# A linear-attention and SwiGLU kernel: the attention's output projection of the last four token tiles as seven block products a pair

## The chip, the cores and the metric

The kernel runs on one core of one Trainium2 chip. The time is device microseconds from the start to the end of one execution; the median of three runs is quoted, with the lowest and the highest. Beside it one execution was recorded by the hardware profiler; its span runs from the first to the last instruction of the program and is a little shorter than the time of that execution. All starts below are microseconds from the start of that span.

Engine names: PE is the matrix engine (PEld its weight loads), DVE the vector engine, ACT the scalar engine, POOL is GpSimd, SP the engine that issues most of the DMAs. ACT issues some DMAs too; these stand in ACT's own stream of instructions, and an instruction that waits holds up all that stand behind it on the same engine.

## The reference

One block of 2048 tokens, width D = 1024, 32 heads of 32, and a feed-forward part with F = 3584:

```python
xn = _layernorm(x)
q, k, v = split(xn @ wqkv)                       # 32 heads of 32
phi = lambda t: where(t > 0, t + 1, exp(t)) + 1e-6
kv = einsum("bhsd,bhse->bhde", phi(k), v)
z  = einsum("bhsd->bhd", phi(k))
o  = einsum("bhqd,bhde->bhqe", phi(q), kv) / (einsum("bhqd,bhd->bhq", phi(q), z) + 1e-6)
s  = o.reshape(B, S, D) @ wo                     # the part that the change touches
g  = silu((silu(xn @ w_gate) * (xn @ w_up)) @ w_down)
return x + s * g
```

Inputs and the output are bfloat16.

## The kernel before

**Stages.** First the layer norm, k, v, q and the sums kv and z. Then a second stage, in the `with` block that opens the pools `wop`, `otp`, `work` and `small`, makes `o` and `s = o @ wo`. Then the feed-forward part (FFN), in which `Group` computes gate and up for 14 blocks of 256 columns, and a last stage that multiplies by `w_down` and writes the output.

**Block products.** Most large products are not done as eight block products of a 2x2 split but as seven (Strassen's scheme in Winograd's form): `part_a` does M3 into a PSUM tile X and M4 into Y, `part_b` does M1 into Z, M5 onto X and M2 onto Y, `part_c` does N7 onto X and N6 onto Y. Each block product is four matmuls of 128x512, all at line 131 (`products`). Between them ACT copies X out (`n` or `qu`), DVE adds Y and Z to it (`q`, `u`), ACT takes the finished off-diagonal blocks out of X and Y, and DVE subtracts N7's X and N6's Y from `u`. The operands are sums of blocks, made beforehand on DVE; for the FFN by `sum_w(m, gu)` (lines 152 to 155, four instructions for each of gate and up of column block m, into `ws_all[:, m % 2, gu]`). `sum_w` needs the raw weights, which `load_w(m)` fetches over SP's queue (lines 177 and 179, 512 KB each for `wg_sb` and `wu_sb`).

**The second stage.** There are 16 token tiles of 128, four to a block b. `emit_ND` computes `o` of one tile (eight small matmuls at line 790, the division on DVE at lines 794 to 800); `emit_OT` writes `o` to DRAM over ACT's queue (line 813) and reads it back transposed over SP's queue (line 814) into `oT_of(b)`: `oT_ab` for blocks 0 and 1, `oT_cd` for blocks 2 and 3, which lies in the storage of `wq_sb` and goes by that name in the trace. `emit_S(b, t, cc)` computes one half row tile of `s`: eight matmuls of 128x512 at line 827 into `s_ps`, an ACT copy to `s_sb` (line 831), and, after the second half, a store to `s_dram` over ACT's queue (line 834). `s_sb` has two buffers. There are 32 such units, u = 0 to 31; `units` and the sets `nd_at`, `row_at` and `q_at` say which other piece is emitted ahead of which unit. `row_at` places the last phi rows (lines 190 and 191, DVE) ahead of units 0 to 9. Ahead of unit 28 stand `sum_w(0, 0)` and `sum_w(0, 1)`, the operands of the first FFN groups. The order in this stage is the order of the code on PE, DVE, ACT, POOL and SP (`manual_schedule`); in the FFN only PE's and POOL's order is that of the code, and a scheduler places DVE's and ACT's instructions, so that instructions of the FFN can come to stand between the last ones of the second stage.

**Behind the last unit.** After the transpose of the last tile `emit_OT` issues the loads of column blocks 0, 1 and 2 of the FFN (`PREF = 3`), six transfers one behind the other on SP's queue. The FFN's first group takes its X, Y and Z from the PSUM space that the second stage leaves (`psF` after `psA` and `psB`; five `psB` tiles take turns). A DMA signals its end through one of eight DMA semaphores that SP's and ACT's transfers share in turn; a transfer that reuses a semaphore waits, on the engine that issues it, until the earlier transfer with that semaphore has landed.

Of the kernel before, what the change touches and what calls it, by code (L numbers as in the profile page):

```python
# [10 lines left out]
ALU = mybir.AluOpType  # L11
FP32 = mybir.dt.float32
# [9 lines left out]
def kernel(  # L22
# [11 lines left out]
    nc = tc.nc  # L34
# [45 lines left out]
    def gate(insts, after, sync=False):  # L80
        if after is None:
            return
        for d in insts:
            tc.add_manual_dep(d.ins, after.ins.name, SYNCD if sync else SCHED, reason="prefetch gate")
# [44 lines left out]
    def products(acc, lhs, rhs, n, first, c0=0, c1=CW):  # L129
        for k in range(n):  # L130
            marks["mm"] = nc.tensor.matmul(acc[:, 0:c1 - c0], lhsT=lhs(k), rhs=rhs(k)[:, c0:c1], start=(first and k == 0),  # L131
                                           stop=(k == n - 1), skip_group_check=True)
# [33 lines left out]
    def sum_w(m, gu):  # L166
        wsum[(m, gu)] = ws_all[:, m % 2, gu]
        for op in wsum_ops(wraw[(m, gu)], wsum[(m, gu)]):
            op()
# [18 lines left out]

    def emit_phi(dst, e):
        nc.vector.tensor_scalar(out=e, in0=e, scalar1=1.0, scalar2=EPS, op0=ALU.min, op1=ALU.add)  # L190
        nc.vector.tensor_tensor(out=dst, in0=e, in1=dst, op=ALU.add)

    p12 = ExitStack()
    wqp = p12.enter_context(tc.tile_pool(name="wqp", bufs=1))
# [16 lines left out]
    class QGroup:  # L211


        def __init__(self, p, m):
            w = wq_sb[:, :, m * FW:(m + 1) * FW]
            self.lhs, self.rhs = block_operands(w, ws_all[:, m // 2, m % 2]), x_operands(p)
            self.out = pqT_tiles[(p, m)]
            self.row = {}

        def mm(self, acc, which, first):  # L220
            products(acc, self.lhs[which], self.rhs[which], HD, first)
# [534 lines left out]
    with ExitStack() as p2:  # L756
        wop = p2.enter_context(tc.tile_pool(name="wop", bufs=1, reuse_waits="tile"))
        otp = p2.enter_context(tc.tile_pool(name="p2oT", bufs=1))
        work = p2.enter_context(tc.tile_pool(name="p2work", bufs=2))
        small = p2.enter_context(tc.tile_pool(name="p2small", bufs=2))  # L760
        oT_ab = otp.tile([P, 2, G, TB], BF16, name="oT")
        oT_cd = wq_sb[:].rearrange("p c n -> p (c n)").rearrange("p (b g t) -> p b g t", b=2, t=TB)
        s_tiles = {}
        wo_sb = wop.tile([P, G, D], BF16, name="wo_sb")

        def oT_of(b):
            return (oT_ab[:] if b < 2 else oT_cd)[:, b % 2]

        def emit_KVZ():
            for j in range(NJ):  # L770
                g0 = j * GPT
                ng = min(GPT, G - g0)
                nc.vector.tensor_tensor(out=KVZ[:, g0:g0 + ng, 0:P], in0=kvz_ps[j][:, 0:ng, 0:P],
                                        in1=mask[:, None, :].to_broadcast([P, ng, P]), op=ALU.mult)
                nc.vector.tensor_tensor(out=KVZ[:, g0:g0 + ng, P:P + HPG],
                                        in0=kvz_ps[j][:, 0:ng, P:P + 1].to_broadcast([P, ng, HPG]),
                                        in1=sel[:, None, :].to_broadcast([P, ng, HPG]), op=ALU.mult)

        def emit_ND(b, t):
            r0 = b * TB + t * P  # L780
            p, t0 = r0 // SP_TOK, r0 % SP_TOK
            nds = []
            rden = small.tile([P, G, HPG], FP32, name="rden", tag="rden")
            for j in range(NJ):
                g0 = j * GPT
                ng = min(GPT, G - g0)
                nd_ps = psA.tile([P, GPT, NDW], FP32, name="nd_ps", tag="A")
                for gi in range(ng):
                    g = g0 + gi
                    mm = nc.tensor.matmul(nd_ps[:, gi, :], lhsT=pqT_tiles[(p, g // 2)][:, g % 2, t0:t0 + P],  # L790
                                          rhs=KVZ[:, g, :], start=True, stop=True)
                    if j == 0 and gi == 0 and t == 0:
                        marks[("ND", b)] = mm
                nc.vector.tensor_scalar(out=rden[:, g0:g0 + ng, :], in0=nd_ps[:, 0:ng, P:P + HPG],
                                        scalar1=EPS, scalar2=None, op0=ALU.add)
                nds.append((g0, ng, nd_ps))
            nc.vector.reciprocal(out=rden[:], in_=rden[:])
            o_sb = work.tile([P, D], BF16, name="o_sb", tag="o_sb", bufs=4)
            for g0, ng, nd_ps in nds:
                nc.vector.tensor_tensor(  # L800
                    out=o_sb[:, g0 * P:(g0 + ng) * P].rearrange("p (g h e) -> p g h e", g=ng, h=HPG),
                    in0=nd_ps[:, 0:ng, 0:P].rearrange("p g (h e) -> p g h e", h=HPG),
                    in1=rden[:, g0:g0 + ng, :, None].to_broadcast([P, ng, HPG, DH]),
                    op=ALU.mult)
            o_ready.append((b, t, o_sb))

        o_ready = deque()

        def emit_OT():
            while o_ready:  # L810
                b, t, o_sb = o_ready.popleft()
                r0 = b * TB + t * P
                nc.scalar.dma_start(out=o_dram[r0:r0 + P, :], in_=o_sb[:])
                nc.sync.dma_start_transpose(out=oT_of(b)[:, :, t * P:(t + 1) * P], in_=o_dram[r0:r0 + P, :])
                if (b, t) == (NB - 1, TPB - 1):
                    for m in range(PREF):
                        load_w(m)

        def emit_S(b, t, cc):
            oT = oT_of(b)  # L820
            ttok = slice(t * P, (t + 1) * P)
            if (b, t) not in s_tiles:
                s_tiles[(b, t)] = work.tile([P, D], BF16, name="s_sb", tag="s_sb")
            s_sb = s_tiles[(b, t)]
            s_ps = psB.tile([P, CW], FP32, name="s_ps", tag="B")
            for c in range(G):
                mm = nc.tensor.matmul(s_ps[:], lhsT=oT[:, c, ttok], rhs=wo_sb[:, c, cc * CW:(cc + 1) * CW],  # L827
                                      start=(c == 0), stop=(c == G - 1))
                if c == 0:
                    marks[("S", b, t, cc)] = mm  # L830
            nc.scalar.copy(out=s_sb[:, cc * CW:(cc + 1) * CW], in_=s_ps[:])  # L831
            if cc == NCC - 1:
                r0 = b * TB + t * P
                nc.scalar.dma_start(out=s_dram[r0:r0 + P, :], in_=s_tiles.pop((b, t))[:])

        PREF = 3
        units = deque((b, t, cc) for b in range(NB) for t in range(TPB) for cc in range(NCC))
        nds = deque((b, t) for b in range(NB) for t in range(TPB))

        def s_unit():  # L840
            emit_S(*units.popleft())

        def nd_tile():
            if nds:
                emit_ND(*nds.popleft())

        with tc.manual_schedule(engines=FRONT_ORDER | {ET.SP}):

            qb, qc = QGroup(NPASS - 1, NM_Q - 2), QGroup(NPASS - 1, NM_Q - 1)
            for c in range(NCC):  # L850
                nc.sync.dma_start(out=wo_sb[:, :, c * CW:(c + 1) * CW], in_=wo_v[:, :, c * CW:(c + 1) * CW])
            emit_KVZ()
            qa.part_b()
            nd_tile()
            qb.part_a()
            emit_OT()
            qa.part_c()
            nd_tile()
            qb.part_b()
            emit_OT()  # L860
            nd_tile()
            qb.part_c()
            emit_OT()


            rows = deque((grp, i) for grp in (qa, qb, qc) for i in range(2))
            nd_at = {1, 2, 4, 6, 8, 10, 11, 13, 15, 16, 17, 19, 20}
            row_at = {0, 1, 3, 5, 7, 9}
            q_at = {0: qc.part_a, 2: qc.part_b, 3: qc.part_c}
            assert len(nd_at) == len(nds) and len(row_at) == len(rows)  # L870
            u = 0
            while units:
                if u in q_at:
                    q_at[u]()
                if u in nd_at:
                    nd_tile()
                if u in row_at:
                    grp, i = rows.popleft()
                    grp.part_d(i)
                if len(units) == 2 * NCC:  # L880
                    sum_w(0, 0)
                    sum_w(0, 1)
                s_unit()
                emit_OT()
                u += 1
    p12.close()
    ps12.close()

# [371 lines left out]
```

## Time and profile before

| | |
|---|---|
| time, median of 3 runs | 748.49 us (748.48 to 748.79) |
| the profiled execution: its time | 748.76 us |
| the profiled execution: its span | 747.0 us |
| granted PE clock | 0.999 of full speed |
| PE busy | 740.2 us, 3708 matmuls |
| DVE, ACT, POOL busy | 509.2, 273.4, 51.2 us |
| the four last token tiles' units, u = 24 to 31 | 219.69 to 233.5 us |
| HBM traffic over the span | 147 GB/s |

Busy times of engines overlap; the span is set by what PE does plus the stretches in which PE waits. A wait in brackets in the profile's lines, such as `[0.48 <-ACT s_sb L831]`, is idle time of that engine just before the instruction, and what ended it. An engine name with a q (SPq, ACTq) marks an instruction that issues a DMA; the time beside it is that of the issue, not of the transfer.

### The profile page before, as it was taken

Reading aid. Unit: us, or ns where it says so; the run is one execution under the profiler, and the core shown is the slowest. Engines: PE = TensorE matmul, PEld = TensorE weight load, DVE = VectorE, ACT = ScalarE, POOL = GpSimd, SP = SyncE. Lnnn points to the kernel's source line nnn. Section 1 sums busy time; section 2 is a strip of 40 time slices with the busy share of each in tenths; the row PEclk is TensorE's granted clock in tenths of the full one; section 3 lists DMA queues with packets and bytes.
Section 4 is the critical chain, followed back from the end, with each engine's and each line's share of the span. In section 5 each row is a group of like instructions: output and inputs, shape, how many; then the busy total and the mean of one; then the engine's idle time right before and its main releaser. Section 6 shows DMA issues by size and latency. Waiting matters only on the chain.

```text
span 747.0 us, 9899 instructions
## 1 busy us (share of the span) xinstructions
PE 740.2 (99%) x3708; PEld 347.8 (47%) x3708; DVE 509.2 (68%) x939; ACT 273.4 (37%) x478; POOL 51.2 (7%) x101
## 2 busy tenths in 40 slices
PE   9999999999999999999999999999999999999997
PEld 4544444455544444444444444444444444444454
DVE  6889896688735767886678867876655744445554
ACT  4444574755234334434343333434342111111111
POOL 3310000000000000000000000000000221121220
PEclk9999999999999999999999999999999999999999
DMA  9756000315799543655336643555879745554200
GB/s 318 253 163 168 1 0 1 113 44 160 195 230 276 148 140 104 185 178 161 103 102 198 190 123 106 152 157 161 260 247 349 291 169 183 183 183 183 85 29 29
DMA packets 132464, 118.09 MB, mean 158 GB/s; under 512 B 33728, under 2 KB 112704, under 8 KB 131136
## 3 DMA queue, kind: packets, MB, share of 16 engines
q1 hardware_dynamic: 127520, 108.68, 46.9%
q10 hardware_dynamic: 4896, 8.78, 3.5%
q8 instruction: 29, 0.48, 0.3%
q14 instruction: 19, 0.16, 0.1%
HBM read 70.52 MB, written 39.58 MB: 147 GB/s over the span
## 4 chain that ended last, share of the span: by engine, by line
PE 97%; DMA 1%; DVE 1%; ACT 0%; issue 0%; ACTq 0%; DVEq 0%
PE X L131 29%; PE Y L131 29%; PE Z L131 10%; PE kv_ps L455 9%; PE s_ps L827 6%; PE qY L131 3%; PE qX L131 3%; PE kY L131 2%; PE kX L131 2%; DMA wg_sb<-in_B_w_gate_dram 1%; PE nd_ps L790 1%; PE kvz L484 1%; PE qZ L131 1%; PE w_ps L493 1%; PE kZ L131 1%; PE tr_ps L411 0%
## 5 line engine op out<-in xcount | busy, mean ns | idle before, releaser
L131 PEld LDWEIGHTS <-ws_all 128*128 128x128 bf16 x1420 | 137.7, 98 | 162.3 <-issue 0.2
L923 DVE TENSOR_TENSOR q<-n,Y 128x512 f32<-128x512 f32 x63 | 43.3, 687 | 106.1 <-PE Y L131 106.1
L131 PEld LDWEIGHTS <-xs 128*128 128x128 bf16 (+1 forms) x736 | 69.6, 98 | 76.5
L1193 POOL TENSOR_TENSOR o_out<-y,xres 128x512 bf16<-128x512 f32 x29 | 35.2, 1213 | 663.3 <-DVE y L1192 663.3
L131 PE MATMUL Y<-xs,ws_all 128*128 128x512 f16 (+3 forms) x308 | 70.3, 360 | 0.0
L131 PE MATMUL X<-xnT,ws_all 128*128 128x512 f16 (+1 forms) x280 | 70.2, 379 | 0.0
L131 PE MATMUL X<-xs,ws_all 128*128 128x512 f16 x224 | 57.5, 379 | 0.0
L131 PE MATMUL Z<-xs,ws_all 128*128 128x512 f16 x224 | 57.5, 379 | 0.0
L131 PE MATMUL Y<-xnT,ws_all 128*128 128x512 f16 x224 | 57.5, 379 | 0.0
L1047 ACT ACTIVATE g<-cg 128x512 bf16<-128x512 f32 x56 | 35.3, 631 | 54.1 <-DVE cg L938 54.0
L929 DVE TENSOR_TENSOR u<-Z,q 128x512 f32<-128x512 f32 x63 | 43.1, 685 | 16.0 <-PE Z L131 15.9
L1047 ACT ACTIVATE g<-X 128x512 bf16<-128x512 f32 x28 | 16.7, 597 | 99.5 <-PE X L131 99.5
L455 PEld LDWEIGHTS <-xnT 128*128 128x128 f16 x320 | 30.7, 98 | 35.8 <-DVE xnT L427 0.5
L919 ACT COPY n<-X 128x512 f32<-128x512 f32 x63 | 36.9, 585 | 28.4 <-PE X L131 27.7
L1072 DVE TENSOR_TENSOR ho<-g,up 128x1024 bf16<-128x1024 bf16 x56 | 38.1, 684 | 0.5
L455 PE MATMUL kv_ps<-wk_sb,xnT 128*128 128x512 bf16 x160 | 37.3, 379 | 0.3 <-DVE xnT L427 0.3
L455 PE MATMUL kv_ps<-wv_sb,xnT 128*128 128x512 bf16 x160 | 36.5, 379 | 0.0
L1192 DVE TENSOR_TENSOR y<-y,s_in 128x512 f32<-128x512 f32 x31 | 22.2, 716 | 20.9 <-ACT y L1186 15.8
L131 PEld LDWEIGHTS <-wg_sb 128*128 128x128 bf16 x224 | 21.9, 98 | 27.1 <-issue 0.8
L131 PEld LDWEIGHTS <-wu_sb 128*128 128x128 bf16 x224 | 21.9, 98 | 26.4
L831 ACT CAST s_sb<-s_ps 128x512 bf16<-128x512 f32 x32 | 18.5, 585 | 40.0 <-PE s_ps L827 36.1
L1186 ACT ACTIVATE y<-X 128x512 f32<-128x512 f32 x8 | 4.8, 597 | 69.7 <-PE X L131 69.7
(179 smaller groups left out, 1132.6 us busy)
## 6 DMA issues: line engine op xcount, KB each, us to landing
h_dram<-ho SPq DMA_DIRECT2D x56, 256.0 KB, 2.6
wg_sb<-in_B_w_gate_dram SPq DMA_DIRECT2D x14, 512.0 KB, 4.1
wu_sb<-in_B_w_up_dram SPq DMA_DIRECT2D x14, 512.0 KB, 4.2
wdr<-in_B_w_down_dram SPq DMA_DIRECT2D x14, 512.0 KB, 4.1
ws_all<-h_dram SPq DMA_DIRECT2D x4, 1792.0 KB, 8.6
wds_dram<-wdsA SPq DMA_DIRECT2D x14, 384.0 KB, 2.7
hp_a<-h_dram SPq DMA_DIRECT2D x3, 1792.0 KB, 8.9
o_dram<-o_sb ACTq DMA_DIRECT2D x16, 256.0 KB, 3.1
```

The lines of the kernel that those rows point to most:

```text
L131: marks["mm"] = nc.tensor.matmul(acc[:, 0:c1 - c0], lhsT=lhs(k), rhs=rhs(k)[:, c0:c1], start=(first and k == 0), stop=(k == n - 1), skip_g ...
L455: mm = nc.tensor.matmul(kv_ps[:], lhsT=xn_tok_ap(i)[:, dc, :], rhs=wkv_ap(c)[:, dc, :], start=(dc == 0), stop=(dc == DC - 1))
L484: nc.tensor.matmul(kvz_ps[j][:, gi, 0:P + 1], lhsT=pk_sb[:, g * P:(g + 1) * P], rhs=v_sb[:, g, 0:P + 1], start=(i == 0 and gi == 0), stop= ...
L827: mm = nc.tensor.matmul(s_ps[:], lhsT=oT[:, c, ttok], rhs=wo_sb[:, c, cc * CW:(cc + 1) * CW], start=(c == 0), stop=(c == G - 1))
L831: nc.scalar.copy(out=s_sb[:, cc * CW:(cc + 1) * CW], in_=s_ps[:])
L919: nc.scalar.copy(out=n[:], in_=self.X[:])
L923: nc.vector.tensor_tensor(out=self.q[:], in0=n[:], in1=self.Y[:], op=ALU.add)
L929: nc.vector.tensor_tensor(out=self.u[:], in0=Z[:], in1=self.q[:], op=ALU.add)
L1047: nc.scalar.activation(out=self.g[:, i, j * TB:(j + 1) * TB], in_=src, func=ACT.Silu)
L1072: nc.vector.tensor_tensor(out=self.ho[:, i], in0=self.g[:, i], in1=self.up[:, i], op=ALU.mult)
L1192: nc.vector.tensor_tensor(out=t[:], in0=t[:], in1=self.s_in[:, i, cs], op=ALU.mult)
L1193: (nc.vector if last and (i, j) != (0, 0) else nc.gpsimd).tensor_tensor(out=self.o_out[:, i, cs], in0=t[:], in1=self.xres[:, i, cs], op=AL ...
```

## The change

The last four token tiles (block 3) are no longer done as eight units but as two pairs of tiles, each pair a 256-row product of seven block products (`SGroup`, with the same three parts as the other groups). A pair's left operands are sums of blocks of `oT`, made on DVE by `sums()` (four instructions a pair); the right operands are sums of blocks of `wo`, made once, on GpSimd, by five instructions of 128x2048, emitted ahead of units 10, 11, 12, 14 and 18 and made to wait for the last phi row (`marks["phi"]`). The sums lie in storage that is free by then: `oT_ab` of blocks 0 and 1, the second half of `ws_all`, and `oT_cd` of block 2. `s_sb` has four buffers in place of two. `sum_w(0, 0)` and `sum_w(0, 1)` move from ahead of unit 28 to behind `part_c` of the first pair and behind `part_c` of the second. `load_at` only renames the place of the loads.

```diff
     def emit_phi(dst, e):
...
-        nc.vector.tensor_tensor(out=dst, in0=e, in1=dst, op=ALU.add)
+        marks["phi"] = nc.vector.tensor_tensor(out=dst, in0=e, in1=dst, op=ALU.add)
...
-                s_tiles[(b, t)] = work.tile([P, D], BF16, name="s_sb", tag="s_sb")
+                s_tiles[(b, t)] = work.tile([P, D], BF16, name="s_sb", tag="s_sb", bufs=4)
...
+        wo_sums = deque((out, u, v, op) for out, (u, v, op) in zip(wos, (
+            (w12, w22, ALU.subtract), (w21, w11, ALU.subtract), (w11, w22, ALU.add), (w21, w22, ALU.add),
+            (w11, w12, ALU.add))))
+        s_rhs = {"M3": wos[0], "M4": wos[1], "M1": wos[2], "M5": w22, "M2": w11, "N7": wos[3], "N6": wos[4]}
...
+        class SGroup:
...
+            def sums(self):
+                o, sm, tt = self.o, self.sum, nc.vector.tensor_tensor
+                a, b = slice(0, P), slice(P, 2 * P)
+                tt(out=self.s1, in0=o[:, 0:HD, a], in1=o[:, HD:DC, b], op=ALU.add)
+                tt(out=sm[:, :, 0:2 * P], in0=o[:, 0:HD, :], in1=o[:, HD:DC, :], op=ALU.add)
+                tt(out=sm[:, :, 2 * P:3 * P], in0=o[:, HD:DC, b], in1=o[:, HD:DC, a], op=ALU.subtract)
+                tt(out=sm[:, :, 3 * P:4 * P], in0=o[:, 0:HD, a], in1=o[:, 0:HD, b], op=ALU.subtract)
...
+            def store(self, i):
+                r0 = ((NB - 1) * TPB + self.t + i) * P
+                nc.scalar.dma_start(out=s_dram[r0:r0 + P, :], in_=self.s[i][:])
+
+            def part_a(self):
+                self.s = [work.tile([P, D], BF16, name="s_sb", tag="s_sb", bufs=4) for _ in range(2)]
+                self.X = psB.tile([P, CW], FP32, name="sX", tag="B")
+                self.mm(self.X, "M3", True)
+                self.u = qtmp.tile([P, CW], FP32, name="qu", tag="qu")
+                nc.scalar.copy(out=self.u[:], in_=self.X[:])
+                self.Y = psB.tile([P, CW], FP32, name="sY", tag="B")
+                self.mm(self.Y, "M4", True)
+                nc.vector.tensor_tensor(out=self.u[:], in0=self.u[:], in1=self.Y[:], op=ALU.add)
+
+            def part_b(self):
+                Z = psB.tile([P, CW], FP32, name="sZ", tag="B")
+                self.mm(Z, "M1", True)
+                nc.vector.tensor_tensor(out=self.u[:], in0=self.u[:], in1=Z[:], op=ALU.add)
+                self.mm(self.X, "M5", False)
+                nc.scalar.copy(out=self.out(0, 1), in_=self.X[:])
+                self.mm(self.Y, "M2", False)
+                nc.scalar.copy(out=self.out(1, 0), in_=self.Y[:])
+
+            def part_c(self):
+                for acc, which, i in ((self.X, "N7", 0), (self.Y, "N6", 1)):
+                    self.mm(acc, which, False)
+                    nc.vector.tensor_tensor(out=self.out(i, i), in0=self.u[:], in1=acc[:], op=ALU.subtract)
+                    self.store(i)
...
+            wo_at = {10, 11, 12, 14, 18}
+            sum_at = {23: lambda: groups[0].sums()}
...
-            while units:
+            n7 = TPB * NCC
+            groups = [SGroup(t) for t in range(0, TPB, 2)]
+            for u in range(len(units) - n7):
...
-                if len(units) == 2 * NCC:
-                    sum_w(0, 0)
-                    sum_w(0, 1)
+                if u in wo_at:
+                    out, a, b, op = wo_sums.popleft()
+                    gate([nc.gpsimd.tensor_tensor(out=out, in0=a, in1=b, op=op)], marks["phi"], sync=True)
+                if u in sum_at:
+                    sum_at[u]()
                 s_unit()
                 emit_OT()
-                u += 1
+            sg, sh = groups
+            sg.part_a()
+            sh.sums()
+            sg.part_b()
+            sh.part_a()
+            sg.part_c()
+            sum_w(0, 0)
+            sh.part_b()
+            sh.part_c()
+            sum_w(0, 1)
```

## The prediction

> **What bounds the kernel now.** Read first were the page's busy times, its slices and its chain of waits.
>
> ```profile
> span 747.0 us, 9899 instructions
> PE 740.2 (99%) x3708; PEld 347.8 (47%) x3708; DVE 509.2 (68%) x939; ACT 273.4 (37%) x478; POOL 51.2 (7%) x101
> ...
> PE 97%; DMA 1%; DVE 1%; ACT 0%; issue 0%; ACTq 0%; DVEq 0%
> ```
>
> PE sets the time: 97% of the chain, at a granted clock of 0.999. So a matmul that goes is worth its place in PE's stream, and a wait of PE costs its length, if nothing later takes it back. Next came the timeline from 200 to 242 us, the end of the second stage and the start of the FFN (columns: start, duration, engine, line, operation, and in brackets the idle time before it and what ended it).
>
> ```profile
> 212.78 20.88 PE L827 MATMUL s_ps<-wo_sb,wq_sb 128*128 128x512 bf16 x96
> ...
> 221.73 0.63 SPq L179 DMA_DIRECT2D wu_sb<-in_B_w_up_dram  x1
> ...
> 223.95 0.33 ACTq L834 DMA_DIRECT2D s_dram<-s_sb  x1
> ...
> 227.32 0.42 DVE L152 TENSOR_TENSOR ws_all<-wg_sb 128x512 bf16<-128x512 bf16 x1 [12.40 <-DMA wg_sb<-in_B_w_gate_dram]
> ...
> 231.04 0.43 DVE L152 TENSOR_TENSOR ws_all<-wu_sb 128x512 bf16<-128x512 bf16 x1 [2.03 <-DMA wu_sb<-in_B_w_up_dram]
> ...
> 231.32 1.07 ACT L831 CAST s_sb<-s_ps 128x512 bf16<-128x512 f32 x2 [3.95 <-DMA s_dram<-s_sb]
> ...
> 233.34 0.43 DVE L152 TENSOR_TENSOR ws_all<-wg_sb 128x512 bf16<-128x512 bf16 x1 [0.60 <-DMA wg_sb<-in_B_w_gate_dram]
> ...
> 233.49 1.03 PE L131 MATMUL X<-xs,wg_sb 128*128 128x512 f16 x4
> ...
> 235.00 1.02 PE L131 MATMUL Y<-xs,wg_sb 128*128 128x512 f16 x4 [0.48 <-ACT s_sb L831]
> ...
> 235.24 0.43 DVE L152 TENSOR_TENSOR ws_all<-wu_sb 128x512 bf16<-128x512 bf16 x1 [0.20 <-DMA wu_sb<-in_B_w_up_dram]
> ...
> 236.86 0.68 DVE L923 TENSOR_TENSOR q<-n,Y 128x512 f32<-128x512 f32 x1
> ...
> 237.59 1.02 PE L131 MATMUL Y<-xnT,ws_all 128*128 128x512 f16 x4
> ```
>
> The reader is to see four things. PE runs through units 20 to 31 without a gap. The weights that the FFN needs arrive only just in time: the four DVE rows at line 152 give the landings of gate 0, up 0, gate 1 and up 1 as 227.3, 231.0, 233.3 and 235.2. ACT was stopped for 3.95 us by a store whose `s_sb` buffer it wanted, and through that PE lost time at the FFN's Y (Y starts 1.51 us after X, where four matmuls take 0.86: 0.65 lost). And the last row above, the FFN's first M2 at 237.59, stands right behind the end of `q` at 237.54, so both PE and DVE's chain from the landing of up 1 end there. I take that M2 as the marker: from there on PE has no gap in the old trace, so its shift is the shift of the span.
>
> **What is removed.** Twelve units take 20.88 us, 1.73 each (the last matmul's tail of 0.16 left off). Eight units are 13.8 us; two pairs are 2 x 7 block products of 0.863, 12.1 us. Gain 1.73. Four `s_sb` buffers take away the wait for the old store; with it the loss of 0.65 at Y goes. If nothing else waited, M2 would stand at 219.69 + 12.08 + 4 x 0.863 = 235.23, 2.36 us earlier.
>
> **What is added on POOL.** Five sums of 128x2048. The nearest row is line 1193, 128x512 in 1213 ns mean, so 4.9 us each; its slowest row took 2.81, so 11.2 as upper bound; below 4 x 1.15 nothing speaks for. I take 4.9. The last phi row ends at 191.06; four sums then end at 210.7, and the fifth, which must also wait for block 1's last unit (203.3), at 215.6. The first use is M3 at 219.69, the last N6 at 226.60. This is hidden, with 9 us and more to spare; where it is not, see below. Contention of POOL with DVE: in the last stage DVE's subtractions from PSUM (line 938) keep about 0.68 us beside POOL, and a sum of two SBUF operands (line 1159) rises from 1.08 to 1.66 in its longest. From 191 to 215 DVE has only the division of `o`, whose large operand is in PSUM; I take nothing.
>
> **What is added on DVE and on the transposes' times.** The sums of a pair are four instructions, by the rows of lines 152 to 155 in pitches of 0.34, 0.60, 0.34 and 0.34. A pair needs its second tile at once, so the transposes count: they landed at 219.63 for tile 1 (issued 214.18, 5.4 us) and 222.9 for tile 3 (issued 219.54, 3.4). Tile 1 is first used by M4 at 220.55, tile 3 at 224.87. Slack 0.9 and 2.0 us: no wait. DVE runs pair 1's sums to 221.3, pair 2's from 222.9 to 224.6, then u + Z, the next u + Y and pair 1's two subtractions, the last one done at 228.3. PE goes on to pair 2's M2 at 229.19 without a wait.
>
> **What is moved, and where the wait goes.** Two queues decide. The first is ACT's. In the built program the store of tile 0 reuses the DMA semaphore of gate 0's load, that of tile 1 up 0's, that of tile 2 gate 1's, that of tile 3 up 1's. Before, up 0's landing held no store. Now the store of tile 1, in ACT's stream ahead of pair 2's two copies out of X and Y, waits for it, and PE's N7 of pair 2 waits for the copy. The second is DVE's. In the built program its order at the border is:
>
> ```
> pair 1: u - X, u - Y
> sum_w gate 0: lines 152 153 154 155
> pair 2: u + Z
> sum_w gate 1: lines 152 153        <- waits for gate 1's load
> pair 2: u - X
> sum_w gate 1: line 154
> pair 2: u - Y
> sum_w up 0: lines 152 153 154 155
> sum_w gate 1: line 155 ; sum_w up 1: line 152
> FFN q (needed by the FFN's first M2)
> ```
>
> So everything down to `q` is queued behind the landing of gate 1; the FFN's Z also waits for u - Y of pair 2.
>
> When do these loads land? The store of tile 0, issued at 223.95 before, can't leave ahead of 227.5 now (it waits for N7's result and for gate 0). It landed after 7.3 us, in the middle of up 0 and gate 1. In 227.3 to 231.0 the DMAs moved 312 GB/s, so 256 KB (0.26 MB) are 0.84 us: up 0 lands at 230.2 and gate 1 at 232.5. If gate 1 follows up 0 as up 1 followed gate 1 (1.9 us), it lands at 232.1. I take 232.3. The ends are 231.6 (the stores of tiles 0 and 1 both out of the way, 233.3 less twice 0.84) and 233.3 (nothing gained).
>
> ACT: store 230.2 + 0.33, copy 0.58 and some 0.1 of hand-over: N7 starts at 231.2, 1.15 later than 230.05. The second stage ends at 232.9 in place of 231.8. DVE from gate 1's landing: 0.34 + 0.60 (lines 152, 153), 0.60 (u - X; pitch of line 938), 0.34, 0.60 (u - Y), 0.34 + 0.60 + 0.34 + 0.34 (up 0), 0.34, 0.34, then `q` 0.68 and 0.05 to PE: 5.5 us. M2 starts at 232.3 + 5.5 = 237.8, against 235.23 with no wait and 237.59 before. The FFN's Z isn't late: u - Y ends at about 234.9, PE is there at 234.7.
>
> **Sum.** +0.2 us on the span of 747.0: the 2.36 of gain are given back, 1.15 at pair 2's N7 and the rest at M2. The profiled execution took 748.76, 0.27 above the median of the runs; the same shift on the median 748.49 gives 748.7. With the two ends of the landing M2 lies at 237.1 and 238.8, that is -0.5 and +1.2: 748.0 to 749.7.
>
> One rule of the Trainium skill bears on the landing. The traced store needed 7.3 us for 256 KB, so it stood behind what SP had already queued. The skill's page "DMA: Bandwidth & Descriptors", section "Queues, rings and completion order", says that each DMA engine takes turns between the rings of SP and ACT, packet by packet; a store would then not stand behind the loads. The traced 7.3 us speak against it, though not strictly.
>
> **Rivals.**
>
> *The stores compete at once.* Mechanism in this kernel: tile 0's store, issued at 227.5, takes its 0.84 us from up 0 and gate 1 just as the old one did, so gate 1 lands at 233.3 as before. M2 at 238.8, +1.2 us: 749.7. For it: stores issued at 212.99 and 217.04 landed in 3.3 and 3.0 us beside other traffic. Against it: the two stores among the loads took 7.3 and 6.2. The Trainium skill's rule of turns, above, would give this one.
>
> *The gain arrives.* M2 near 235.2 to 236: 746.1 to 746.9. It needs gate 1 to land before 230.6 and up 0 before 229.5, each 1.5 us or more earlier than in the old trace, or another order on DVE than the built one. For it: PE's stream is otherwise free, and the loads lose a competitor. Against it: 1.57 MB ahead of that landing, of which only 0.26 to 0.5 MB can get out of the way.
>
> *Slower.* One mechanism: gate 1's load lands later than before, because both stores of pair 1 (0.5 MB, 1.7 us of DMA) now fall in the same 3 us as it, at 227.5 and 230.2, where before the first was spread over 7 us. From 233.6 on the kernel is slower by over 1.5 us, and each us later costs one us; at 234 to 235 M2 is at 239.5 to 240.5: +1.9 to +2.9, 750.4 to 751.4. For it: DVE has no way round that landing. Against it: SP issues the loads earlier than these stores.
>
> *POOL too slow.* At 11.2 us a sum the fourth ends at 235.9 and the fifth at 247.1, where N6 wants it at 226.6: 20 us, some 769. It decides from 8.7 us a sum (four sums between 191.06 and N7 at 225.73). Only the first POOL instruction of that kind in the last stage took so long.
>
> That the products aren't saved is no rival: the built program has eight matmuls less.
>
> **Chances.** Forecast 0.48, stores compete at once 0.13, gain arrives 0.19, slower 0.17, POOL 0.03. A change of 0.2%, 1.5 us, is about what a measurement of this kernel tells from none. The first two lie within it (0.61), faster has 0.19, slower 0.20. The likeliest's own range is 748.0 to 749.7; 8 in 10 needs most of the case that gains and the near half of the slower one: 746.3 to 750.7.
>
> **What would show it.** In the new trace: ACT idle until about 230.2 for a DMA of `wu_sb` and N7 of pair 2 late behind it; DVE idle ahead of line 152 on the second `wg_sb`, and M2 of the FFN at its landing plus 5.5. POOL's five sums done by 216. It would be wrong if PE waits for POOL, if M4 or pair 2's M3 wait for a transpose, or if DVE reaches `q` by 235.

## The result and the profile after

The changed kernel takes 747.89 us (median of 22 runs, 747.15 to 748.88) where the kernel before, run beside it, takes 748.92 (748.34 to 749.57). The ratio is 0.9986, with an interval of 0.998 to 0.9993: 0.14% faster, or 1.0 us. The forecast was +0.2 us, the range 746.3 to 750.7. So the time is inside the wide range, but just below the likeliest case's own (748.0 to 749.7). It is within 0.2% of no change, but the sign is the other one, and the interval lies wholly below 1. Of the 1.73 us that the products promised, and of the 2.36 with the waits, 1.0 came through.

First the page of the changed kernel: its span, the busy times and the shares of the chain of waits.

```profile
span 746.2 us, 9886 instructions
...
PE 736.9 (99%) x3661; PEld 347.0 (47%) x3700; DVE 517.4 (69%) x955; ACT 272.3 (36%) x476; POOL 69.9 (9%) x106
...
PE 96%; DMA 2%; DVE 1%; issue 0%; ACT 0%; DVEq 0%; ACTq 0%
```

PE still sets the time. Weight loads fell from 3708 to 3700, the eight matmuls saved (of the matmul records of this trace 39 are missing). POOL is busy for 19 us more.

Then the timeline of the changed kernel around the border of the two stages (start, duration, engine, line, operation; in brackets the idle time before it and what ended it).

```profile
219.91 1.03 PE L131 MATMUL sX<-oT,wq_sb 128*128 128x512 bf16 x4
...
227.78 1.83 ACTq L884 DMA_DIRECT2D s_dram<-s_sb  x2
227.88 0.69 DVE L908 TENSOR_TENSOR s_sb<-qu,sY 128x512 bf16<-128x512 f32 x1 [0.17 <-PE sX L131]
...
229.40 1.03 PE L131 MATMUL sY<-wo_sb,wq_sb 128*128 128x512 bf16 x4
...
229.71 0.58 ACT L901 CAST s_sb<-sX 128x512 bf16<-128x512 f32 x1 [3.83 <-PE sX L131]
...
230.34 1.02 PE L131 MATMUL sX<-ws_all,wq_sb 128*128 128x512 bf16 x4
...
231.30 0.42 DVE L152 TENSOR_TENSOR ws_all<-wg_sb 128x512 bf16<-128x512 bf16 x1 [0.53 <-DMA wg_sb<-in_B_w_gate_dram]
231.64 0.68 DVE L153 TENSOR_TENSOR ws_all<-wg_sb 128x1024 bf16<-128x1024 bf16 x1
...
232.07 1.03 PE L131 MATMUL X<-xs,wg_sb 128*128 128x512 f16 x4
232.24 0.68 DVE L908 TENSOR_TENSOR s_sb<-qu,sX 128x512 bf16<-128x512 f32 x1
...
232.93 1.03 PE L131 MATMUL Y<-xs,wg_sb 128*128 128x512 f16 x4
...
233.18 0.68 DVE L908 TENSOR_TENSOR s_sb<-qu,sY 128x512 bf16<-128x512 f32 x1
...
233.91 1.02 PE L131 MATMUL Z<-xs,ws_all 128*128 128x512 f16 x4
...
234.94 1.02 PE L131 MATMUL X<-xnT,ws_all 128*128 128x512 f16 x4
...
236.05 0.68 DVE L1011 TENSOR_TENSOR q<-n,Y 128x512 f32<-128x512 f32 x1
...
236.79 1.02 PE L131 MATMUL Y<-xnT,ws_all 128*128 128x512 f16 x4 [0.83 <-DVE q L1011]
```

Read it from the bottom. The FFN's first M2 is at 236.79, with PE idle for 0.83 us ahead of it, for `q` on DVE. Going up DVE's column, `q` ends a run without a gap that begins at 231.30 with the first sum of gate 1, and that one was released by the DMA of `wg_sb`. The busy time of each engine in that stretch says the same (window, length, then busy time and instructions of PE, PEld, DVE, ACT and POOL, TensorE's granted clock, DMA share, GB/s):

```profile
231.30:236.79 5.49, 4.66 (x22) 1.85 (x21) 5.49 (x13) 2.46 (x3) 0.00 (x0) 1.00 1.13 337
```

DVE is busy for 5.49 of 5.49 us, PE for 4.66. This is the chain that the prediction wrote down, at its length (5.5). What came out otherwise is the time at which it begins.

The whole change of the span can be read between two marks: the start of the last four tiles on PE and that M2. Before: 219.69 to 237.59, 17.90 us. After: 219.91 to 236.79, 16.88 us. The difference, 1.02 us, is close to that of the medians, 1.03, but the agreement is in part chance: two further profiles of the kernel before, below, have 17.57 and 17.27 between these marks, and a second one of the changed kernel 16.67, so a single pair of profiles gives anything from 0.4 to 1.2. The size of the gain is that of the medians; the marks show where it lies. The other 0.2 between the two profiled spans (747.0 and 746.2) lies ahead of the first mark, where executions of one kernel differ as well (219.7 to 220.1 in the three of the kernel before). From M2 to the end both take 509.4 us, so nothing is taken back later. PE without any wait would need 12.08 + 3.45 = 15.53 us between the marks. So the changed kernel loses 1.35 there: 0.08 at pair 2's N7 (230.34), 0.12 and 0.17 at the FFN's Z and the X behind it, 0.99 at M2 (each the distance of two starts less 0.863).

Last, the groups of POOL's instructions, in the view by lines of the changed kernel (busy us, mean ns, then the idle time before them):

```profile
L959 POOL TENSOR_TENSOR oT<-wo_sb 128x2048 bf16<-128x2048 bf16 x3 | 12.2, 4072 | 147.2 <-DVE pqT L191 147.2
L959 POOL TENSOR_TENSOR ws_all<-wo_sb 128x2048 bf16<-128x2048 bf16 x2 | 8.1, 4082 | 0.0
```

The five sums of `wo` take 4.07 us each and end at 211.5, over 8 us ahead of the last four tiles.

### The profile page after: what moved, and what is told of

Read it like the earlier page. It is cut to its first block, busy times and chain, and to the rows that moved or that the text cites. A ratio compares the mean times of both kernels' runs of the same rounds, so it can differ in the third digit from the quotient of the medians.

```text
span 746.2 us, 9886 instructions
## 1 busy us (share of the span) xinstructions
PE 736.9 (99%) x3661; PEld 347.0 (47%) x3700; DVE 517.4 (69%) x955; ACT 272.3 (36%) x476; POOL 69.9 (9%) x106
## 4 chain that ended last, share of the span: by engine, by line
PE 96%; DMA 2%; DVE 1%; issue 0%; ACT 0%; DVEq 0%; ACTq 0%
PE X L131 29%; PE Y L131 29%; PE Z L131 10%; PE kv_ps L455 9%; PE s_ps L829 5%; PE qX L131 3%; PE qY L131 3%; PE kY L131 2%; PE kX L131 2%; DMA wg_sb<-in_B_w_gate_dram 1%; PE nd_ps L790 1%; PE kvz L484 1%; PE qZ L131 1%; PE kZ L131 1%; DMA xp<-in_A_x_dram 0%
## 5 line engine op out<-in xcount | busy, mean ns | idle before, releaser
L829 PE MATMUL s_ps<-wo_sb,oT 128*128 128x512 bf16 x123 | 29.0, 379 | 0.2
```

## The experiments

The theory under test: the chain of DVE behind gate 1's landing is all that stands between the changed kernel and 15.53 us, and the landing itself varies between executions. Rivals: the stores of pair 1 among the loads set the landing; the four row tiles are the gain, or a part of it; POOL's sums take time from DVE or PE.

### The changed kernel again

Nothing is edited.

> The changed kernel once more, as the neighbour of the next three. Theory (the gain is cut by DVE's chain, which waits for the load of gate 1): the FFN's first M2 starts 5.5 us behind the landing of gate 1, wherever that falls; with a landing between 231 and 233 M2 is at 236.6 to 238.5 and the span 746.0 to 747.9. Rival (M2 is bound by PE's own stream or by the pairs' own work): M2 keeps its distance to the end of the second stage, 4.7 us behind the start of X, and does not follow the landing.

747.47 us (11 runs), ratio 0.9983, interval 0.9974 to 0.9992. In its profile gate 1 lands at 231.00 and M2 stands at 236.58, again 5.58 behind the landing, and 16.67 behind the first mark. So the sign is no accident of one job, and M2 follows the landing as expected.

### FFN's sums of gate 1 and later behind the first u

The sums that the FFN makes one step ahead (for the step after its first one) are held back until the first step's `u` is computed, so that on DVE they no longer stand ahead of pair 2's subtractions and `q`.

```
-    def sum_w(m, gu):
+    def sum_w(m, gu, after=None):
...
-            op()
+            gate([op()], after)
...
-            nc.vector.tensor_tensor(out=self.u[:], in0=Z[:], in1=self.q[:], op=ALU.add)
+            marks["u"] = nc.vector.tensor_tensor(out=self.u[:], in0=Z[:], in1=self.q[:], op=ALU.add)
...
-                    sum_w(m + 1, gu)
+                    sum_w(m + 1, gu, marks["u"] if m == 0 else None)
```

> The sums of gate 1 and up 1 are placed on DVE behind the u of the FFN's first and second group; nothing else changes. Theory: DVE no longer waits for gate 1 ahead of q; M2 stands at PE's own place, 235.5 to 235.8 with landings as in the profile after, and the span is 744.9 to 745.2, 1.0 to 1.3 us below the changed kernel; if up 1 lands as late as 235 the store of the last row tile holds ACT's copy n and M2 is still late, up to 237. Rival: no difference to the changed kernel, 746.2.

746.79 us (9 runs), ratio 0.9974, interval 0.9965 to 0.9984: 1.9 us faster than before by the ratio, and the profiled span is 744.6. Against the changed kernel in the same job (747.47) the medians differ by 0.7 us, and the two intervals overlap; the clear evidence is in the trace. Its timeline at the border:

```profile
231.06 0.69 DVE L908 TENSOR_TENSOR s_sb<-qu,sX 128x512 bf16<-128x512 f32 x1 [0.56 <-PE sX L131]
...
234.14 0.68 DVE L1011 TENSOR_TENSOR q<-n,Y 128x512 f32<-128x512 f32 x1
...
235.18 1.03 PE L131 MATMUL Y<-xnT,ws_all 128*128 128x512 f16 x4
...
235.56 0.42 DVE L152 TENSOR_TENSOR ws_all<-wg_sb 128x512 bf16<-128x512 bf16 x1
```

The first row shows it: u - X of pair 2 now waits for PE and no longer behind a load. `q` ends at 234.8, 0.4 ahead of PE, and M2 carries no bracket: PE didn't wait. From the first mark (219.63) to M2 it is 15.55 us, the 15.53 without waits. Gate 1 landed at 230.79 here, much as in the changed kernel (231.21 and 231.00; counted from the first mark 11.16, 11.30 and 11.09), so it's the order on DVE that lets this load cost anything. This is the fastest kernel of the study, together with the one that adds the next edit to it.

### Pair stores on SP

The four stores of the last pairs are issued by SP in place of ACT, so that ACT's copies out of PSUM stand behind no store.

```
-                nc.scalar.dma_start(out=s_dram[r0:r0 + P, :], in_=self.s[i][:])
+                nc.sync.dma_start(out=s_dram[r0:r0 + P, :], in_=self.s[i][:])
```

> The pairs' four stores of s are issued by SP in place of ACT; DVE's order stays. Theory: ACT no longer waits for landings, so N7 of pair 2 and M5 of the FFN's first group start without a wait (0.1 to 0.3 us in the profile after), but M2 still follows gate 1's landing by 5.5 us: the span stays within 0.3 us of the changed kernel at equal landing. Rival (ACT's stores are what holds PE): 1 us or more faster.

747.91 us (11 runs), ratio 0.9987, interval 0.9979 to 0.9996: as the changed kernel. The timeline of this run:

```profile
232.36 0.42 DVE L152 TENSOR_TENSOR ws_all<-wg_sb 128x512 bf16<-128x512 bf16 x1 [0.77 <-DMA wg_sb<-in_B_w_gate_dram]
...
234.97 1.02 PE L131 MATMUL Z<-xs,ws_all 128*128 128x512 f16 x4 [0.59 <-DVE s_sb L908]
...
237.85 1.02 PE L131 MATMUL Y<-xnT,ws_all 128*128 128x512 f16 x4 [0.99 <-DVE q L1011]
```

The first row to the last is 5.49 us once more. ACT's queue is out of it (the FFN's X stands 12.09 behind the first mark, so the 0.08 is gone), and nothing is gained: M2 still follows the first sum of gate 1.

### Both

The two edits above together.

> Both: gate 1's and up 1's sums behind u, and the stores on SP. Theory: no wait for a load is left ahead of M2, it stands at 235.2 to 235.5 whatever the landings, the span is 744.7 to 745.0, about 2.1 to 2.3 us below the kernel before, and the runs spread less than those of the changed kernel. Rival: something else takes the gain, the span stays above 745.7.

746.99 us (6 runs), ratio 0.9971, interval 0.996 to 0.9983; first mark to M2 15.54 us. It can't be told from the kernel with DVE's edit alone. The profiled span, 745.6, misses the 744.7 to 745.0 expected; the excess is ahead of the first mark, which stands at 220.65. Once DVE is out of the way, the stores on ACT cost nothing that shows.

### Four row tiles alone

On the kernel before, only the number of row buffers for S is changed; the products stay as they were.

```
-                s_tiles[(b, t)] = work.tile([P, D], BF16, name="s_sb", tag="s_sb")
+                s_tiles[(b, t)] = work.tile([P, D], BF16, name="s_sb", tag="s_sb", bufs=4)
```

> The kernel before with four s_sb buffers in place of two, nothing else. As the prediction put it: the loss of 0.65 us ahead of the FFN's Y goes, the span falls by 0.65. Rival: ACT's store of tile 2 waits for gate 1's landing all the same (its DMA semaphore is that load's), the last two casts stand behind it and Y waits for the last cast as before: no gain, Y 0.5 us late.

748.46 us (10 runs), ratio 0.9998, interval 0.9988 to 1.0007: no change that can be measured, where 0.65 was expected. Its timeline:

```profile
228.56 0.43 DVE L152 TENSOR_TENSOR ws_all<-wu_sb 128x512 bf16<-128x512 bf16 x1
...
231.60 0.43 DVE L152 TENSOR_TENSOR ws_all<-wg_sb 128x512 bf16<-128x512 bf16 x1 [1.34 <-DMA wg_sb<-in_B_w_gate_dram]
...
234.57 1.03 PE L131 MATMUL X<-xs,wg_sb 128*128 128x512 f16 x4
...
235.44 1.03 PE L131 MATMUL Y<-xs,wg_sb 128*128 128x512 f16 x4
```

X to Y is 0.87 us: the loss of 0.65 is away, and first mark to M2 is 17.28 where 13.82 + 3.45 = 17.27 is the least. But a loss that the other runs of the kernel before don't have every time (below) is worth little when it is removed. The rival cause, ACT's store of tile 2 waiting for gate 1's landing, isn't tested by this run: gate 1 was in at 231.58, and that store left at 231.93.

This run also bears on the failed step. Its stores left at 225.03 and 228.48, on the old plan, with the first of them among the loads, and all the same up 0 landed 6.3 us after its issue and gate 1 8.7. In the changed kernel, whose first store of a pair left only at 227.78, they took 7.4 and 9.5 us. So the store of tile 0 isn't what had held the loads in the first profile, where they took 9.3 and 10.9.

### Two row tiles in the changed kernel

```
-                s_tiles[(b, t)] = work.tile([P, D], BF16, name="s_sb", tag="s_sb", bufs=4)
+                s_tiles[(b, t)] = work.tile([P, D], BF16, name="s_sb", tag="s_sb", bufs=2)
...
-                self.s = [work.tile([P, D], BF16, name="s_sb", tag="s_sb", bufs=4) for _ in range(2)]
+                self.s = [work.tile([P, D], BF16, name="s_sb", tag="s_sb", bufs=2) for _ in range(2)]
```

> The changed kernel with two s_sb buffers in place of four. Theory: pair 2's copies out of X and Y wait until the stores of pair 1 have landed (233.6 and 235.0 in the profile after), N7 moves to about 234.2 and N6 to 235.6; M2 at about 240, span some 3.5 us above the changed kernel. Rival (the buffers do not matter, since the loads hold M2 anyway): within 0.5 us of the changed kernel.

753.63 us (4 runs), ratio 1.0068, interval 1.0051 to 1.0085; the span is 752.1, 5.9 over that of the changed kernel. Two rows of its timeline:

```profile
234.38 0.59 ACT L901 CAST s_sb<-sX 128x512 bf16<-128x512 f32 x1 [8.68 <-DMA s_dram<-s_sb]
...
235.02 1.86 PE L131 MATMUL sX<-ws_all,wq_sb 128*128 128x512 bf16 x4 [4.76 <-ACT s_sb L901]
```

With two buffers pair 2's copies wait for pair 1's store to land, ACT stands for 8.68 us and PE for 4.76. So in the changed kernel the four buffers are needed: a pair fills two rows at once, and the next pair wants two more. The direction was as expected, the size larger, for a reason in the last section: the 1.86 us in the second row, where the same four matmuls take 1.03 elsewhere.

### The sums of wo on DVE

```
-                    gate([nc.gpsimd.tensor_tensor(out=out, in0=a, in1=b, op=op)], marks["phi"], sync=True)
+                    nc.vector.tensor_tensor(out=out, in0=a, in1=b, op=op)
```

> The five sums of wo are made by DVE at the same places, 1.14 us each, in place of GpSimd. Theory: they lie beside PE's S units either way; the transposes of block 3 may land up to 1 us later and that is hidden behind the loads: within 0.5 us of the changed kernel. Rival (GpSimd takes time from DVE through their shared port, and the change pays for that): 0.5 to 1 us faster than the changed kernel.

747.97 us (10 runs), ratio 0.9992, interval 0.9982 to 1.0001. The sums take 1.2 us each on DVE, and they stand ahead of the division of `o` there. One row of the timeline of PE:

```profile
204.62 1.09 PE L790 MATMUL nd_ps<-KVZ,pqT 128*128 128x132 bf16 x8
```

In the changed kernel this group takes 0.77. The view of waits puts 0.8 us of idle weight loads in this run down to DVE's `o_sb`; from the first `s_ps` to the first mark PE takes 52.74 us here and 52.36 in the kernel before and in the changed one. So GpSimd as the place is worth some 0.4 us, and the equal 52.36 shows that POOL's sums cost PE nothing there. They cost DVE nothing either: the division's 128x384 rows at that time take 0.55 us in the mean in all three, beside POOL or not. The rival didn't come true. The two time intervals overlap; the 0.4 rests on one profile.

### Gate 1 loaded last

SP issues the three prefetched loads in the order 0, 2, 1.

```
-        load_at = {(NB - 1, TPB - 1): range(PREF)}
+        load_at = {(NB - 1, TPB - 1): (0, 2, 1)}
```

> The changed kernel with the loads of column blocks 1 and 2 in exchanged order, so that gate 1 is the fifth transfer in place of the third and lands near 235.8. Theory: M2 5.5 us behind that landing, at 241.3, the span 4 to 4.5 us above the changed kernel. Rival: M2 does not follow gate 1; within 0.5 us.

751.93 us (4 runs), ratio 1.0044, interval 1.0029 to 1.0059; the span is 750.2. The timeline:

```profile
234.62 0.43 DVE L152 TENSOR_TENSOR ws_all<-wg_sb 128x512 bf16<-128x512 bf16 x1 [3.57 <-DMA wg_sb<-in_B_w_gate_dram]
...
237.23 1.02 PE L131 MATMUL Z<-xs,ws_all 128*128 128x512 f16 x4 [2.82 <-DVE s_sb L908]
...
238.26 1.87 PE L131 MATMUL X<-xnT,ws_all 128*128 128x512 f16 x4
...
239.38 0.68 DVE L1011 TENSOR_TENSOR q<-n,Y 128x512 f32<-128x512 f32 x1
...
240.11 1.72 PE L131 MATMUL Y<-xnT,ws_all 128*128 128x512 f16 x4
```

Gate 1's first sum is 3.32 us later than in the changed kernel, and M2, again 5.49 behind it, 3.32 as well. So each microsecond of that landing costs one, in the direction of later too. Another 0.7 is lost behind M2 (510.1 us to the end in place of 509.4): M2's four matmuls take 1.55 to the next start, where 0.86 is usual. The landing itself, 234.53, came 1.3 earlier than the 235.8 expected; that the span still rose by the 4.0 expected is owed to this 0.7, which the expectation did not have.

### The kernel before, profiled twice more

Nothing is edited.

> The kernel before, profiled once more. Theory (the late landings of up 0 and gate 1 in the first profile came from one of the 16 DMA engines in that execution, not from the program): up 0 lands within 7 us and gate 1 within 9.5 us of its issue, in place of 9.3 and 10.9; the FFN's Y follows X after 0.86 us, with no loss. Rival (the store of tile 0 among the loads is what delays them, as the prediction put it): 9 and 10.5 us or more, and Y late again.

> The kernel before, profiled a third time: the same expectations as for the second profile. If the three differ in landing, so that one shows the loss at Y and another not, the loss is a matter of the execution.

One run each, 748.73 and 748.59 us; the spans are 747.0 and 746.8. The same two rows of the timeline, in the first of them:

```profile
231.62 0.43 DVE L152 TENSOR_TENSOR ws_all<-wg_sb 128x512 bf16<-128x512 bf16 x1 [2.03 <-DMA wg_sb<-in_B_w_gate_dram]
...
234.96 1.02 PE L131 MATMUL Y<-xs,wg_sb 128*128 128x512 f16 x4
```

And in the second:

```profile
230.74 0.43 DVE L152 TENSOR_TENSOR ws_all<-wg_sb 128x512 bf16<-128x512 bf16 x1 [0.60 <-DMA wg_sb<-in_B_w_gate_dram]
...
234.82 1.03 PE L131 MATMUL Y<-xs,wg_sb 128*128 128x512 f16 x4
```

Gate 1 has its first sum at 231.62 and 230.74, where the profile of the prediction had 233.34. Up 0 landed at 227.88 and 228.42, there at 231.02. Counted from their issues, up 0 took 6.7 and 7.5 us and gate 1 9.9 and 8.8, where it was 9.3 and 10.9: each run misses one of the two bounds expected (7 and 9.5), and neither fits the rival on both. The loss at Y is 0.30 (234.96, with X at 233.80 and 0.86 for its four matmuls) and none, where it was 0.65. The program is the same in all three.

## Why the prediction came out as it did

**The step that failed is "When do these loads land?"** It took the landings of one execution, 231.0 and 233.3, for those of the program, and put their lateness down to one cause, the store of tile 0 in their midst, with 0.84 us to be had from moving it. Up 0 landed at 228.50, not 230.2, and gate 1 at 231.21, not 232.3 and outside the two ends given, 231.6 and 233.3. Counted from the first mark, gate 1 was 1.31 us earlier than forecast (11.30 against 12.61) and M2 was 1.23 earlier (16.88 against 18.11). That is the whole error in the stretch. Two other runs of the kernel before and the one with four row tiles alone, all with the old products, had gate 1 at 230.72 to 231.60: the execution that the prediction read was the late one.

The semaphore increments in the traces say how it was late. Each load raises its semaphore in 16 steps, and lands with the last. In that execution 15 of the 16 were in for up 0 at 228.57 and the last at 231.02; for gate 1 the two times are 231.01 and 233.32. In the changed kernel the last one is 0.09 and 0.97 behind. From the first mark to gate 1's landing it is 13.63 us in the one and 11.30 in the other, and the 2.33 between them are 1.34 of this last step and 0.92 of a later issue (2.73 and 1.81 behind the mark); the 15 others took 8.59 and 8.52 from the issue. In the other profiles of the kernel before the load was issued 1.7 and 1.8 behind the mark, so the issue, too, was late in that one execution. The 15 others took about as long in both, so it was not the number of bytes ahead of them. What held the last part isn't shown. An instruction fetch of 16 KB runs at 227.07 in the late execution, in the midst of up 0; but one runs at 226.46 in the second further profile and at 227.27 with four row tiles alone, also within up 0's time, and there the last step of up 0 came 0.10 and 0.22 behind the others. So the fetch alone doesn't explain it.

**ACT's queue: 1.15 at pair 2's N7.** This wait did not come about, and its sign, ACT idle for a DMA of `wu_sb`, is not in the trace. Up 0 landed at 228.50, 1.7 us earlier than forecast, and the store of tile 1 left at 228.64, right behind u - Y (227.88 + 0.69 = 228.57), the row that it stores. In the second profile of the changed kernel it left at 228.64 too, with up 0 landed at 228.35. What is left is 0.08: the two issues on ACT end at 229.61, and the copy out of X begins at 229.71. Why the second issue takes 0.97 us there, where it takes 0.33 in the run with the sums behind `u`, isn't shown. The term hangs on the failed step; whether a late up 0 would have cost 1.15 here, no run of the changed kernel shows.

**DVE's queue: landing plus 5.5.** Right: from the landing 5.58, and 5.49 from the first sum, in the changed kernel, with the stores on SP, and with gate 1 last. The run that moves the sums behind `u` shows it to be the cause of the loss that remained: with nearly the same landing all of it goes.

**The gain of 1.73 by the products.** Right: without waits 17.27 before and 15.53 after, and both values were seen (17.28 and 15.55).

**The 0.65 at Y.** Taken for a part of the program, and put down to a row buffer alone. Two more rows of the trace that it read, the kernel before:

```profile
233.40 0.38 ACTq L834 DMA_DIRECT2D s_dram<-s_sb  x1
...
233.88 1.07 ACT L831 CAST s_sb<-s_ps 128x512 bf16<-128x512 f32 x2 [1.48 <-PE s_ps L827]
```

The FFN's Y waits for the second of these casts. Their buffer was free at 233.56, with the landing of tile 1's store, but they stand behind the issue of tile 2's store, which left only at 233.40: its data were there at 232.39, and it reuses the semaphore of gate 1's load, which landed at 233.32. So by this trace late gate 1 ended the wait there, and four buffers alone would not have removed it; no run tests that. In the first further profile gate 1 was in time, and there the buffer did cost 0.30: the casts began at 233.84, behind a store that landed at 233.76. The loss was 0.65, 0.30 and 0 in three executions, and four buffers alone gave a ratio of 0.9998. Measured from the other two executions, 17.57 and 17.27 between the marks, a forecast of 2.36 to be gained has 2.0 and 1.7 in it. This error runs the other way than that of the landing.

**POOL, the transposes, M2 as the marker.** POOL's sums took 4.07 us in place of 4.9, less than the 4.6 below which nothing was said to speak for, and stayed hidden; the row that gave the price reads f32, these read bf16. The last four transposes landed at 214.70, 216.99, 221.49 and 222.75, and PE waited for none. M2's distance to the end is 509.4 us before and after.

**The rivals.** *The stores compete at once* gave 749.7, by holding gate 1 at 233.3. Pair 1's stores, issued at 227.78 and 228.64, landed after 5.8 and 6.4 us, where those of before took 7.3 and 6.2, and gate 1 came earlier; it is not what happened. The Trainium skill's rule of turns ("DMA: Bandwidth & Descriptors", section "Queues, rings and completion order") isn't refuted by that, since a store that takes turns with loads may be this slow too; no run here tells the two apart. *The gain arrives* came in part: it needed gate 1 before 230.6, and got 231.2. By the order on DVE, its other condition, it arrives in full. *Slower* and *POOL too slow* did not happen; run with gate 1 last, the kernel is slower in the way that *Slower* describes, though by the order of the loads and not by stores.

## What to carry to other kernels

Before a sum is built on when a load lands, read that landing in several executions; a row with a bracket of DMA in one profile is one draw, and here the last sixteenth of a load came 2.4 us late in the one execution that was read, and the baseline and the forecast were both taken from it. When a change takes work from the engine that bounds, look next at what the scheduler has queued on the helper engines ahead of the first consumer: sums for a later step stood in front of the subtractions that the present step waited for, and ordering them behind it was worth another 0.7 us by the medians of one job, and 1.1 to 1.3 in the stretch that the traces show. Buffers that do nothing alone (four row tiles, ratio 0.9998) can be what the rest of a change stands on (with two, 1.0068).

## What was not expected of the hardware

In two runs here a wait of PE cost more than its length. These are windows of the run with two row tiles (columns as in the window above; TensorE's granted clock is the third number from the end):

```profile
230.30:235.00 4.70, 0.00 (x0) 0.00 (x0) 0.73 (x2) 0.59 (x1) 0.00 (x0) 0.81 1.15 332
235.00:236.70 1.70, 1.68 (x5) 0.56 (x5) 0.99 (x2) 0.59 (x1) 0.00 (x0) 0.50 0.99 240
236.70:238.40 1.70, 1.70 (x6) 0.58 (x5) 0.73 (x2) 0.00 (x0) 0.00 (x0) 0.50 1.00 281
238.40:240.10 1.70, 1.70 (x6) 0.58 (x5) 1.47 (x3) 0.00 (x0) 0.00 (x0) 0.50 0.55 186
240.10:241.80 1.70, 1.70 (x9) 0.78 (x8) 1.70 (x6) 1.49 (x2) 0.00 (x0) 1.00 0.45 167
```

After 4.76 us without a matmul the granted clock is 0.50 for 5.1 us, and the three groups in it take 1.7 us each in place of 0.86: 2.5 us on top of the wait. The record of the clock has it at half from 233.26, within the wait, to 240.09. With that the 5.9 us of this run are understood, where the wait alone had been reckoned. In the run with gate 1 last 2.82 us of idleness were enough: the first group behind it still ran at full rate, and then the clock was 0.50 from 238.13 to 241.54, 3.4 us. The Trainium skill describes this on its page "TensorE: Matmul & The Clock Gate", in "Part 1: The HAM clock gate": half clock after an idle window of about 3.4 us, full clock again after as long a busy one. The 3.4 us at half clock in the run with gate 1 last agree, while the 5.1 us of work at half clock in the other run are more; the idle time that sufficed, 2.82 us, is less than that figure, and the measurement decides.
